# A two-layer MLP tail on TensorE: the output product moved out of the unit loop and done as seven Strassen passes

## The chip, the cores and the metric

The kernel runs on one core of one Trainium2 chip. Times are device microseconds of one execution; three runs of the kernel before are shown below. TensorE is the matmul engine, VectorE (DVE in the profile), ScalarE (ACT) and GpSimd (POOL) are the elementwise engines, SyncE (SP) issues all DMAs. All data is float32; the matmuls read operands of type float32r.

## The reference

```python
attn = coarse attention on 4-fold means, repeated, + banded local attention
x = attn as (2304 tokens, 512)
a = x @ w1; b = x @ w2                  # 512 -> 1024
h = a * b @ w3                          # 1024 -> 1024
y = h @ w_out                           # 1024 -> 512, first MLP
h2 = y @ w_in                           # 512 -> 2048
g = h2 * (1.0 / (1.0 + np.exp(-h2)))    # silu
out = g @ w_out2                        # 2048 -> 512
```

The change concerns the last three lines: `y`, 2304 tokens by 512, with `w_in` (512 by 2048) and `w_out` (2048 by 512) of the second MLP, called `w_in` and `w_out` from here on.

## The kernel before, in words

Every product of float32 accuracy is three matmuls (`PASSES`): each operand is split into a rounded high part (a cast to float32r) and a residual (operand minus high part, an elementwise subtraction of two SBUF operands), and high x high, residual x high and high x residual are added up in PSUM.

Up to about 109 us an opening written out by hand (`OPENING`) runs attention for the first heads and prepares the first weights. Then a list of `slots` is run, TensorE in that written order: groups of `ab` products (x with w1 and w2), `y` products, and the rest of attention between them. `y` is stored to DRAM (`ydram`). Beside it, 16 background units (`bg_steps`, lines 808 to 864; `plan` gives each step a slot) prepare `w_in` and `w_out` for the last stage: load, join two 32-bit words into one float, for `w_in` also form four Strassen sums (`mix`), cast to a high part (`high`, line 833), subtract (`rest`, line 837) and store both parts to DRAM (`wsd`, `wod`). In this part only TensorE's order is fixed by hand; steps on the other engines are put behind given instructions.

The last stage (lines 1003 to 1159) is written in a fixed order for all engines. Tokens come in `NT = 3` slabs of 768 (index `t`), two halves of 384 each; the 2048 middle columns in 8 blocks of 256 (index `p`). There are 24 units `u = 8 t + p`. `h_unit(u)` (line 1090) does one 2 x 2 Strassen product of a slab with a block of `w_in`: seven products (`CH`), each six matmuls of 384 columns, that is two contraction tiles times three passes. The operands of y are four blocks of the slab and four sums of them (`y_mix`, on GpSimd, line 919), cast on ScalarE (`y_high`, line 924) and with a residual on VectorE or GpSimd (`y_rest`, line 930). The operands of `w_in` are loaded per unit, already split (`wc_load`, lines 940 and 943). Each of the seven products starts a PSUM bank afresh; VectorE adds them up into `cf` and `cg` (line 1098), ScalarE takes the sigmoid (line 1063), VectorE multiplies and casts (lines 1069, 1072), GpSimd subtracts (line 1074). That gives `g` as two parts.

Between the products of a unit stand the output blocks of the unit before (`run_out`, `out_block`, line 1011): six blocks of 128 tokens times two halves, each three matmuls of 512 columns (line 1021) with `w_out` as the moving operand, added up over all p in six PSUM banks per slab. At the end of a slab the six banks are copied and stored (lines 1033 to 1041). The next slab of y is loaded in p = 1, mixed in p = 2 to 5, split in p = 7.

Products of the y sums to PSUM banks, and banks to engines, in the kernel before:

```python
            bank = s_tile if u or i == 6 else mm_tile if i < 4 else t_tile
            acc_full = bank(f"h{u}_{i}")
```

Of the kernel before, what the change touches and what calls it, by code (L numbers as in the profile page):

```python
# [8 lines left out]
F32 = mybir.dt.float32  # L9
# [65 lines left out]
def tile_model(ctx: ExitStack, tc: tile.TileContext, qk, vw, vr, w12, w3t, wo, wb, out):  # L75
# [14 lines left out]
    s_cb, s_late = ExitStack(), ExitStack()  # L90
# [5 lines left out]
    wsd = tc.dram_tile([8, P, 3584], F32, name="wsd")  # L96
    wod = tc.dram_tile([8, P, 2048], F32, name="wod")
# [710 lines left out]
    def bg_steps(n):  # L808
# [18 lines left out]
        def high(w):  # L827
            home = stg
            if late:
                n_res[0] += 1  # L830
                home = (stg, late[0])[n_res[0] % 2]
            hold["r"] = home.tile([P, 2, 1024], F32R, tag="res", name="res", bufs=1)[:, :, :w]
            nc.scalar.copy(hold["r"][:, 0], hold["f"][:, :w])

        def rest(w):
            r = hold["r"]
            nc.vector.tensor_tensor(
                out=r[:, 1], in0=hold["f"][:, :w], in1=r[:, 0].bitcast(F32), op=ALU.subtract
            )

        def store(where):
            nc.sync.dma_start(
                where.rearrange("p (l n) -> p l n", l=2), hold["r"].bitcast(F32)
            )

        def mix():
            f = hold["f"]
            a11, a12, a22, a21 = (f[:, 256 * i:256 * i + 256] for i in range(4))
            for out_, in0, in1, op in (
                (a22, a21, a22, ALU.add), (a21, a11, a21, ALU.subtract),  # L850
                (a11, a22, a11, ALU.subtract), (a12, a12, a11, ALU.subtract),
            ):
                nc.vector.tensor_tensor(out=out_, in0=in0, in1=in1, op=op)

        steps = [(0, first), (1, clamp), (3, low), (4, lambda: bg_load(n + 2))]
        if kind:
            steps += [(4, lambda: high(1024)), (5, lambda: rest(1024)),
                      (6, lambda: store(wod[p]))]
        else:
            steps += [(4, lambda: high(768)), (5, lambda: rest(768)),  # L860
                      (6, lambda: store(wsd[p, :, 0:1536])), (6, mix),
                      (8, lambda: high(1024)), (9, lambda: rest(1024)),
                      (10, lambda: store(wsd[p, :, 1536:3584]))]
        return steps
# [9 lines left out]
    late, n_res = [], [0]  # L874
# [13 lines left out]
    Y, YC, WC, WO, G, OUT = {}, {}, {}, {}, {}, {}  # L888

    CH = (("b11", 0, 0), ("b21", 0, 1), ("t2", 1, 0), ("t1", 1, 2),  # L890
          ("b22", 1, 1), ("t3", 1, 3), ("t4", 0, 2))
# [20 lines left out]
    def y_mix(t, i):  # L912
        b = Y[t]
        out_, in0, in1 = (("t1", "b12", "b11"), ("t2", "b22", "t1"),
                          ("t3", "b22", "b12"), ("t4", "t2", "b21"))[i]
# [18 lines left out]
    def wc_load(u):  # L934
        if u >= NUN:
            return
        p = u % 8
        t3 = wpool.tile([P, 2, 3, 256], F32R, tag="wB", name=f"wca{u}")
        t4 = wpool.tile([P, 2, 4, 256], F32R, tag="wB", name=f"wcb{u}")
        nc.sync.dma_start(  # L940
            t3.rearrange("p l c n -> p (l c n)").bitcast(F32), wsd[p, :, 0:1536]
        )
        nc.sync.dma_start(
            t4.rearrange("p l c n -> p (l c n)").bitcast(F32), wsd[p, :, 1536:3584]
        )
        WC[u] = (t3, t4)

    def wo_load(p):
        t = wpool.tile([P, 2, 2, 512], F32R, tag="wA" if p < 4 else "wC", name=f"wo{p}")
        nc.sync.dma_start(t.rearrange("p l f n -> p (l f n)").bitcast(F32), wod[p])  # L950
        WO[p] = t
# [6 lines left out]
    def open_y():  # L958
        s_late.close()
        s_stg.close()  # L960
        yp.append(pool(ctx, "yp", "left"))
        y_load(0)
# [4 lines left out]
    for i, k in ((0, 1), (1, 2), (3, 3), (2, 6), (4, 7), (5, 9), (6, 12)):  # L967
        at(bg_end + k, lambda i=i: y_high(0, i))
        at(bg_end + k + 1, lambda i=i: y_rest(0, i, True))
    at(end_b + 1, lambda: wc_load(0))  # L970
    at(end_b + 2, lambda: wc_load(1))
# [12 lines left out]
    with tc.manual_schedule(engines={T.PE}):  # L984
        for i, slot in enumerate(slots):
# [5 lines left out]
            if not opened and beat[0] >= END:  # L991
                assert not table and not [n for n in ops if n[0] != "z"], (table, list(ops))
                s_att.close()
                late.append(pool(s_late, "late", "left"))
# [221 lines left out]
```

## Time and profile before

| | |
|---|---|
| median of 3 runs | 838.88 us (836.98 to 840.41) |
| span of the profiled execution, first to last instruction | 834.7 us |
| an own device time of the profiled execution | not recorded; the median lies 4.2 us above its span |
| busy: TensorE / VectorE / ScalarE / GpSimd | 99% / 59% / 36% / 32% |
| last stage, from the first product with w_in | from about 453.6 us to the end |
| DMA | 149 MB in 44,032 packets, mean 179 GB/s |

Lines such as L1021 are lines of the kernel before. PE is TensorE's matmuls, PEld its weight loads, which run beside them; a matmul's duration holds its drain, which the next one overlaps, so back to back the spacing is less than the mean duration. An SPq row is a DMA being issued by SP.

### The profile page before, as it was taken

What the parts mean: (1) busy time and instruction counts of PE and PEld (TensorE: products, weight loads), DVE (VectorE), ACT (ScalarE), POOL (GpSimd) and SP (SyncE); (2) the same over time, 40 slices, a digit from 0 to 9 for tenths busy, and PEclk for the clock granted to TensorE, in tenths of its full rate; (3) what the DMA queues carried; (4) which work ended last, traced back from release to release, by engine and by line L of the source; (5) the groups of instructions that cost most, each with busy time, mean ns of one, the idle gap of its engine ahead of it and who ended that gap; (6) DMA issues with size and microseconds to landing.
All of it is one profiled execution on the core that took longest, in us unless ns stands there. A gap on an engine that the chain in (4) does not pass through costs nothing.

```text
span 834.7 us, 17445 instructions
## 1 busy us (share of the span) xinstructions
PE 824.6 (99%) x7126; PEld 736.5 (88%) x7126; DVE 494.4 (59%) x827; ACT 302.1 (36%) x881; POOL 269.6 (32%) x216
## 2 busy tenths in 40 slices
PE   8999999999999999999999999999999999999997
PEld 4555799999999999999999989989989989989986
DVE  7989896666747545476761534438534437534434
ACT  6588664544444534443331211123111123111111
POOL 3000233543535334231451523435223435222220
PEclk9999999999999999999999999999999999999999
DMA  9978754455565724429932864633863423823402
GB/s 313 377 202 265 232 170 153 146 200 189 167 227 165 253 96 165 145 92 332 375 130 75 296 248 146 225 134 97 243 164 95 170 90 97 242 90 95 170 2 75
DMA packets 44032, 149.16 MB, mean 179 GB/s; under 512 B 9136, under 2 KB 15792, under 8 KB 37808
## 3 DMA queue, kind: packets, MB, share of 16 engines
q1 hardware_dynamic: 43952, 148.05, 52.6%
q8 instruction: 56, 0.92, 0.5%
q14 instruction: 24, 0.20, 0.1%
HBM read 115.52 MB, written 32.51 MB: 177 GB/s over the span
## 4 chain that ended last, share of the span: by engine, by line
PE 92%; DMA 4%; DVE 3%; issue 1%; ACT 0%; SPq 0%; ACTq 0%
PE o L1021 24%; PE ab L665 23%; PE h L1110 21%; PE y L733 12%; PE wp L621 4%; PE ol L509 2%; DMA st<-w 2%; DMA qk<-qk 1%; PE s L402 1%; PE td L427 1%; PE od L487 1%; PE tl L457 1%; DMA lent<-wo 1%; PE sd L360 1%; DVE dec L191 0%
## 5 line engine op out<-in xcount | busy, mean ns | idle before, releaser
L1021 PE MATMUL o<-wo,g 128*128 128x512 f32 x864 | 221.1, 393 | 0.0
L1021 PEld LDWEIGHTS o<-wo,g 128*128 128x128 f32 x864 | 160.7, 188 | 25.4
L1074 POOL TENSOR_TENSOR g<-sg,g 128x768 fp32r<-128x768 f32 x46 | 84.9, 1845 | 228.4 <-DVE g L1072 206.8
L1110 PE MATMUL h<-yc,wcb 128*128 128x384 f32 x576 | 116.0, 337 | 0.0
L1110 PEld LDWEIGHTS h<-yc,wcb 128*128 128x128 f32 x576 | 103.2, 188 | 7.7
L707 POOL TENSOR_TENSOR c<-cf,c 128x320 fp32r<-128x320 f32 (+1 forms) x64 | 74.3, 1161 | 102.1 <-DVE c L702 95.9
L733 PE MATMUL y<-c,w_wC 128*128 128x320 f32 (+1 forms) x768 | 106.6, 296 | 0.0
L665 PE MATMUL ab<-x,w_wA 128*128 128x320 f32 (+1 forms) x768 | 106.3, 296 | 0.2 <-DVE w_wA L268 0.2
L665 PE MATMUL ab<-x,w_wB 128*128 128x320 f32 (+1 forms) x768 | 105.7, 296 | 0.0
L665 PEld LDWEIGHTS ab<-x,w_wB 128*128 128x128 f32 x768 | 102.1, 188 | 1.3 <-issue 0.4
L665 PEld LDWEIGHTS ab<-x,w_wA 128*128 128x128 f32 x768 | 101.6, 188 | 1.0 <-DVE w_wA L268 0.5
L733 PEld LDWEIGHTS y<-c,w_wC 128*128 128x128 f32 x768 | 101.9, 188 | 0.3
L1063 ACT ACTIVATE sg<-cf 128x768 f32<-128x768 f32 x24 | 20.3, 847 | 182.8 <-DVE cf L1098 182.8
L1110 PE MATMUL h<-yc,wca 128*128 128x384 f32 x432 | 83.1, 336 | 0.0
L1110 PEld LDWEIGHTS h<-yc,wca 128*128 128x128 f32 x432 | 76.6, 188 | 3.8
L683 DVE TENSOR_TENSOR cf<-ab,af 128x320 f32<-128x320 f32 (+1 forms) x64 | 28.9, 452 | 57.0 <-PE ab L665 37.0
L621 PE MATMUL wp<-w_wo,w_w 128*128 128x512 f32 x128 | 60.1, 602 | 0.3 <-DVE w_wo L191 0.2
L471 POOL TENSOR_TENSOR vr<-vr 72x512 f32<-72x512 f32 x11 | 16.0, 1454 | 120.0 <-DVE w_wB L268 84.1
L1063 ACT ACTIVATE sg<-cg 128x768 f32<-128x768 f32 x24 | 20.3, 847 | 88.3 <-DVE cg L1098 88.3
L1098 DVE TENSOR_TENSOR u<-h,u 128x384 f32<-128x384 f32 x48 | 26.6, 554 | 39.2 <-PE h L1110 39.0
L327 ACT ACTIVATE band<-band,sml 128x38 f32<-128x38 f32 x144 | 44.9, 319 | 5.3 <-DVE sml L418 5.2
L677 ACT COPY af<-ab 128x320 f32<-128x320 f32 (+1 forms) x64 | 25.3, 396 | 53.1 <-PE ab L665 53.0
(124 smaller groups left out, 1007.2 us busy)
## 6 DMA issues: line engine op xcount, KB each, us to landing
wcb<-wsd SPq DMA_DIRECT2D x24, 1024.0 KB
wca<-wsd SPq DMA_DIRECT2D x24, 768.0 KB
sw<-wb SPq DMA_DIRECT2D x32, 512.0 KB
qk<-qk SPq DMA_DIRECT2D x16, 579.0 KB
wsd<-res SPq DMA_DIRECT2D x8, 1024.0 KB
wod<-res SPq DMA_DIRECT2D x8, 1024.0 KB
wo<-wod SPq DMA_DIRECT2D x8, 1024.0 KB
st<-w SPq DMA_DIRECT2D x14, 512.0 KB
```

Of the source, the lines that this page charges most:

```text
L327: nc.scalar.activation(E[:, j, :], src[j], AF.Exp, bias=z[:, j:j + 1], scale=scale, accum_out=z[:, NQB + j:NQB + j + 1],)
L621: nc.tensor.matmul(wp_ps[half, j], lhsT=w3v[:, k, j * P:(j + 1) * P], rhs=wov[:, k, :], start=(gp == 0 and k == 0), stop=(gp == 3 and k == 1),
L665: nc.tensor.matmul(acc[:, :N], lhsT=wv[:, i, w, kk, :], rhs=X[b, h, kk][:, j, :], start=(n == 0), stop=(n == 11),)
L677: mark(nc.scalar.copy(af, C.pop(("ab", b, h, m, 0))[:, :N]))
L683: nc.vector.tensor_tensor(out=cf, in0=C.pop(("ab", b, h, m, 1))[:, :N], in1=C.pop(("af", b, h, m)), op=ALU.mult)
L707: mark(nc.gpsimd.tensor_tensor(out=c[:, 1], in0=C.pop(("cf", b, h, m)), in1=c[:, 0].bitcast(F32), op=ALU.subtract))
L733: nc.tensor.matmul(acc[:, :N], lhsT=WP[kf // 2][:, i, kf % 2, ec * P:(ec + 1) * P], rhs=c[:, j, :], start=(kf == 0 and n == 0), stop=(kf = ...
L1021: nc.tensor.matmul(acc, lhsT=g[:, a, j * P:(j + 1) * P], rhs=w[:, b, half, :], start=(p == 0 and half == 0 and n == 0), stop=(p == 7 and h ...
L1063: nc.scalar.activation(sg, c, AF.Sigmoid)
L1074: e.tensor_tensor(out=g[:, 1], in0=sg, in1=g[:, 0].bitcast(F32), op=ALU.subtract)
L1098: nc.vector.tensor_tensor(out=out_, in0=in0, in1=in1, op=op)
L1110: nc.tensor.matmul(acc, lhsT=wc[w][:, a, c, kt * P:(kt + 1) * P], rhs=y[:, b, kt, :], start=(n == 0), stop=(n == 5),)
```

## The change

The last stage becomes two parts.

First part: the 24 units run without output blocks between them. The seven products of a unit use three PSUM banks: products 0, 2, 4, 6 add into one (`X_`), 3 and 5 into another (`Y_`), 1 has a third (`Z_`); between them ScalarE or VectorE reads the running sum. The silu results `cf`, `cg` stay unsplit and are stored to DRAM (`gd`), with four sums of them that GpSimd makes (`S1` to `S4`, 384 columns each). `w_in` is stored unsplit by the background units and loaded once: 14 tiles of 1024 columns, each cast on ScalarE (`wc_high`) and subtracted on GpSimd (even) or VectorE (odd) (`wc_rest`). Tiles 0 to 3 are split before the last stage, 4 to 13 in units 0 to 5.

Second part: for each of seven Strassen passes, nine tiles of 128 rows; a tile is 24 matmuls of 256 columns. Operands are loaded unsplit (`a_load`, eight tiles ahead; `b_load`) and split on ScalarE and VectorE or GpSimd (`a_split`, four tiles ahead; `b_split`). Partial sums stand in SBUF (`U`, `oa`, `ob`); VectorE adds each pass to them. The first splits of this part stand in units 21 to 23. The pool `late` goes; `w_out` and `w_in` are stored unsplit (`store_plain`, `store_mixed`).

The core of the diff, in the order of the file:

```diff
-        def high(w):
...
-        def rest(w):
...
+        def mix(part):
+            q = [hold["f"][:, 256 * i:256 * i + 256] for i in range(4)]
...
+            for out_, in0, in1, op_ in todo[2 * part:2 * part + 2]:
+                nc.vector.tensor_tensor(out=out_, in0=in0, in1=in1, op=op_)
...
-    for i, k in ((0, 1), (1, 2), (3, 3), (2, 6), (4, 7), (5, 9), (6, 12)):
+    for i, k in ((0, 1), (1, 2), (3, 3), (2, 6), (5, 7), (4, 9), (6, 12)):
...
-    at(end_b + 1, lambda: wc_load(0))
-    at(end_b + 2, lambda: wc_load(1))
+    for s in range(8):
+        k = end_b + 1 + s // 2 if s < 4 else end_a + 1 + s // 4 - 1
+        at(k, lambda s=s: wc_load(s))
+        if s < 4:
+            at(k + 2, lambda s=s: wc_high(s))
+            at(k + 3, lambda s=s: wc_rest(s))
...
+    def halves(t, e):
+        def high():
+            nc.scalar.copy(t[:, 0], t[:, 1].bitcast(F32))
+        def rest():
+            e.tensor_tensor(
+                out=t[:, 1], in0=t[:, 1].bitcast(F32), in1=t[:, 0].bitcast(F32), op=ALU.subtract
+            )
+        return high, rest
...
+    def wc_rest(s, e=None):
+        halves(WC[s], e or (nc.vector if s % 2 else nc.gpsimd))[1]()
...
     def y_rest(t, i, e=None):
         d = YC[t, i]
+        e = e or (nc.vector if i % 2 else nc.gpsimd)
...
+        for i, (name, o) in enumerate(CH):
+            acc = (X_, Z_, X_, Y_, X_, Y_, X_)[i]
...
             if i == 0:
+                nc.scalar.copy(p1, X_)
             elif i == 1:
+                tt(cf[:, first], Z_, p1)
             elif i == 2:
+                nc.scalar.copy(u2, X_)
             elif i == 3:
+                nc.scalar.copy(p5, Y_)
             elif i == 4:
+                tt(cg[:, second], X_, p5)
+                nc.scalar.activation(sg[:, second], cg[:, second], AF.Sigmoid)
             elif i == 5:
+                tt(cf[:, second], Y_, u2)
+                nc.scalar.activation(sf, cf, AF.Sigmoid)
+                tt(cg[:, second], cg[:, second], sg[:, second], ALU.mult)
+                save(2, cg[:, second])
             else:
+                nc.scalar.activation(sg[:, first], X_, AF.Sigmoid)
+                tt(cf, cf, sf, ALU.mult)
+                tt(cg[:, first], X_, sg[:, first], ALU.mult)
...
+                tt(S1, cf[:, second], cg[:, second], ALU.add, g)
+                tt(S3, cf[:, first], cf[:, second], ALU.subtract, g)
+                tt(S2, S1, cf[:, first], ALU.subtract, g)
...
+                tt(S4, cg[:, first], S2, ALU.subtract, g)
...
+            for fn in extra.get(i, ()):
+                fn()
...
+            if t == 0:
+                todo = {0: (4, 5), 1: (6,), 2: (7, 8), 3: (9, 10), 4: (11, 12), 5: (13,)}
+                for k, s in enumerate(todo.get(p, ())):
+                    put((0, 3)[k], lambda s=s: wc_high(s), lambda s=s: wc_rest(s))
+            if t + 1 < NT:
+                if p == 1:
+                    put(6, lambda t=t: y_load(t + 1))
+                if 2 <= p < 6:
+                    put(6, lambda t=t, p=p: y_mix(t + 1, p - 2))
+                if p == 6:
+                    for i in range(2):
+                        put((0, 3)[i], lambda t=t, i=i: y_high(t + 1, i),
+                            lambda t=t, i=i: y_rest(t + 1, i))
+                if p == 7:
+                    for i in range(2, 7):
+                        put(i - 2, lambda t=t, i=i: y_high(t + 1, i),
+                            lambda t=t, i=i: y_rest(t + 1, i))
...
+            elif p == 5:
+                put(0, lambda: b_split(0, 0))
+                put(3, lambda: b_split(0, 1))
+                put(6, lambda: a_load(3), lambda: b_load(1))
+            elif p == 6:
+                put(0, lambda: a_split(0))
+                put(3, lambda: a_split(1))
+                put(6, lambda: a_load(4), lambda: a_load(5))
+            elif p == 7:
+                put(0, lambda: a_split(2))
+                put(3, lambda: a_split(3))
...
+        for m in range(7 * NP):
+            i, n = divmod(m, NP)
...
+            for p in range(8):
+                for k, (a, b) in enumerate(PASSES):
+                    nc.tensor.matmul(
+                        acc, lhsT=A[:, a, p, :], rhs=B_[i][p // 4][:, b, p % 4, :],
...
+            a_load(m + 8)
...
+            a_split(m + 4)
```

## Rows read from the trace of the kernel before

**Rows 1.** The page, busy time of the engines and share of the span
```profile
PE 824.6 (99%) x7126; PEld 736.5 (88%) x7126; DVE 494.4 (59%) x827; ACT 302.1 (36%) x881; POOL 269.6 (32%) x216
```

**Rows 2.** The chain that ended last, in order of time: start, length, work
```profile
433.99 8.48 PE ab L665 x72
442.47 11.31 PE y L733 x96
453.78 11.52 PE h L1110 x66
...
819.88 9.64 PE o L1021 x42
```

**Rows 3.** What TensorE waited for from 109 us on: total us, times, longest
```profile
PE ab L665 <- DVE w_wA L268: 0.2, 1, 0.2
```

**Rows 4.** Three unit periods, busy time of the instructions on h alone
```profile
508.08:523.74 15.66, 8.33 (x43) 7.51 (x43) 3.80 (x7) 0.48 (x1) 1.00 0.50 185
523.74:539.40 15.66, 8.33 (x43) 7.51 (x43) 3.79 (x7) 0.48 (x1) 1.00 0.52 187
539.40:555.06 15.66, 8.33 (x43) 7.51 (x43) 3.80 (x7) 0.48 (x1) 1.00 0.50 183
```

**Rows 5.** TensorE's widths: two timeline rows, then the busy PE, PEld of y
```profile
442.31 11.47 PE L733 MATMUL y<-c,w_wC 128*128 128x256 f32 x96
819.72 9.79 PE L1021 MATMUL o<-wo,g 128*128 128x512 f32 x42
442.31:453.62 11.31, 11.31 (x96) 11.26 (x96) 1.12 (x3) 1.00 0.07 25
```

**Rows 6.** Instructions by line and shape: busy us, mean ns
```profile
L1021 PE MATMUL o<-wo,g 128*128 128x512 f32 x864 | 221.1, 393 | 0.0
L1117 ACT COPY p<-h 128x384 f32<-128x384 f32 x24 | 11.5, 481 | 21.3 <-PE h L1110 21.3
L833 ACT CAST res<-dec 128x1024 fp32r<-128x1024 f32 x16 | 16.8, 1051 | 21.7 <-DVE dec L853 9.3 <-DMA wsd<-res 9.1 <-DVE res L837 2.4
L924 ACT CAST yc<-yr 128x768 fp32r<-128x768 f32 x12 | 9.7, 834 | 0.4 <-PE h L1110 0.4
L683 DVE TENSOR_TENSOR cf<-ab,af 128x256 f32<-128x256 f32 x32 | 13.4, 418 | 30.3 <-PE ab L665 18.0 <-PE tl L457 6.0 <-ACT dec L174 3.9
L539 POOL TENSOR_TENSOR x<-xf,x 128x256 fp32r<-128x256 f32 x11 | 8.5, 768 | 3.7 <-ACT x L535 3.7
```

**Rows 7.** Timeline at the start of the last stage
```profile
453.62 2.25 PE L1110 MATMUL h<-yc,wca 128*128 128x384 f32 x12
454.91 0.48 ACT L1117 COPY p<-h 128x384 f32<-128x384 f32 x1 [0.68 <-PE h L1110]
```

**Rows 8.** Timeline of the opening, a releaser's end and TensorE's start
```profile
23.31 1.23 DVE L191 SCALAR_TENSOR_TENSOR w_wo<-w_wo,lent 128x1024 int32<-128x1024 int32 x1
24.59 4.56 PE L621 MATMUL wp<-w_wo,w_w 128*128 128x512 f32 x10
```

**Rows 9.** Timeline of VectorE and of GpSimd, 412 to 414 and 566 to 575 us
```profile
412.52 1.22 DVE L837 TENSOR_TENSOR res<-dec,res 128x1024 fp32r<-128x1024 f32 x1
566.02 0.96 DVE L1069 TENSOR_TENSOR sg<-cf,sg 128x768 f32<-128x768 f32 x1
567.72 1.84 POOL L1074 TENSOR_TENSOR g<-sg,g 128x768 fp32r<-128x768 f32 x1 [7.10 <-DVE g L1072]
567.96 0.55 DVE L1098 TENSOR_TENSOR cg<-h,u 128x384 f32<-128x384 f32 x1
569.52 1.85 POOL L930 TENSOR_TENSOR yc<-t,yc 128x768 fp32r<-128x768 f32 x1
569.83 2.35 DVE L930 TENSOR_TENSOR yc<-t,yc 128x768 fp32r<-128x768 f32 x1
571.33 2.56 POOL L930 TENSOR_TENSOR yc<-yr,yc 128x768 fp32r<-128x768 f32 x1
572.11 2.60 DVE L1069 TENSOR_TENSOR sg<-cg,sg 128x768 f32<-128x768 f32 x1
```

**Rows 10.** DMA in two stretches: last columns the DMA share and GB/s
```profile
607.00:611.00 4.00, 4.00 (x22) 3.58 (x21) 0.71 (x2) 0.00 (x0) 0.00 (x0) 1.00 1.34 218
414.00:422.00 8.00, 8.00 (x62) 8.00 (x61) 2.17 (x6) 0.80 (x2) 2.97 (x4) 1.00 1.01 379
```

**Rows 11.** Timeline of the end, the last eviction
```profile
829.55 0.69 DVE L1033 COPY last<-o 128x512 f32<-128x512 f32 x1 [0.69 <-PE o L1021]
```

**Rows 12.** GpSimd's residuals of g, one line: durations min/median/max in ns
```profile
L1074 POOL TENSOR_TENSOR g<-sg,g x46: 1834/1846/1860, 463.1 to 807.5; 128x768 fp32r<-128x768 f32 x46
```

More of the change, by code (lines that the diff above doesn't have):

```diff
@@ L841, in store @@
[L841 to L863, printed above, removed]
@@ L864, in bg_steps @@
-        return steps
+        def mix(part):
+            q = [hold["f"][:, 256 * i:256 * i + 256] for i in range(4)]
+            if part == 0:
+                hold["r"] = stg.tile([P, 4, 256], F32, tag="res", name="res", bufs=2)
+            r = [hold["r"][:, i, :] for i in range(4)]
+            if kind:
+                todo = (
+                    (r[0], q[1], q[0], ALU.subtract), (r[1], q[3], r[0], ALU.subtract),
+                    (r[2], q[3], q[1], ALU.subtract), (r[3], q[2], r[1], ALU.subtract),
+                )
+            else:
+                todo = (
+                    (r[2], q[3], q[2], ALU.add), (r[3], q[0], q[3], ALU.subtract),
+                    (r[0], r[2], q[0], ALU.subtract), (r[1], q[1], r[0], ALU.subtract),
+                )
+            for out_, in0, in1, op_ in todo[2 * part:2 * part + 2]:
+                nc.vector.tensor_tensor(out=out_, in0=in0, in1=in1, op=op_)
@@ L866, in tile_model @@
+        return [
+            (0, first), (1, clamp), (3, low), (4, lambda: bg_load(n + 2)),
+            (4, lambda: mix(0)), (5, store_plain), (5, lambda: mix(1)), (6, store_mixed),
+        ]
     plan = {}
@@ L1090, in h_unit @@
[L1090 to L1106 removed]
+    b2.append(pool(ctx, "b2", "right", bufs=2))
@@ new lines, in rows, with store_out, temp @@
+    def rows(t, k):
+        return [64 * ORDER[SEQ[t][2 * k + i]] for i in range(2)]
+    def store_out(o, t, k, c0, c1):
+        r0, r1 = rows(t, k)
+        if r1 == r0 + 64:
+            nc.sync.dma_start(out[r0:r0 + 128, c0:c1], o)
+            return
+        nc.sync.dma_start(out[r0:r0 + 64, c0:c1], o[:64, :])
+        nc.sync.dma_start(out[r1:r1 + 64, c0:c1], o[64:, :])
+    def temp(tag, u, width=NH, bufs=1):
+        return b2[0].tile([P, width], F32, tag=tag, name=f"{tag}{u}", bufs=bufs)
@@ new lines, in h_unit, with b_load, a_load @@
+            for fn in extra.get(i, ()):
+                fn()
+    PR = ((0, 0), (1, 1), (4, 4), (3, 3), (5, 5), (6, 2), (2, 6))
+    NP = 9
+    A_, B_ = {}, {}
+    def b_load(i):
+        B_[i] = []
+        for k in range(2):
+            t = wpool.tile([P, 2, 4, 256], F32R, tag="wB", name=f"wo{i}_{k}")
+            nc.sync.dma_start(
+                t[:, 1].bitcast(F32), wod[:, 4 * k:4 * k + 4, PR[i][1], :]
+            )
+            B_[i].append(t)
+    def a_load(m):
+        if m >= 7 * NP:
+            return
+        i, n = divmod(m, NP)
+        t, j = divmod(n, 3)
+        d = wpool.tile([P, 2, 8, P], F32R, tag="wA" if m % 8 < 4 else "wC", name=f"ga{m}")
+        nc.sync.dma_start(
+            d[:, 1].bitcast(F32), gd[PR[i][0]][t][:, :, j * P:(j + 1) * P]
+        )
+        A_[m] = d
@@ L1150, in tile_model, with a_split, b_split @@
+    def a_split(m):
+        if m < 7 * NP:
+            high, rest = halves(A_[m], nc.vector if m % 2 else nc.gpsimd)
+            high()
+            rest()
+    def b_split(i, k):
+        high, rest = halves(B_[i][k], nc.vector)
+        high()
+        rest()
     E = mybir.EngineType
     with tc.manual_schedule(engines={E.PE, E.DVE, E.Activation, E.Pool, E.SP}):
+        for s in range(8, 14):
+            wc_load(s)
         for u in range(NUN):
-            h_unit(u)
-            assert not todo
@@ L1155, in tile_model, with put @@
-            todo.extend((u, half, j) for half in range(2) for j in range(6))
-        for _ in range(3):
-            next_chain()
-        assert not later
-        run_out(12)
+            t, p = divmod(u, 8)
+            ex = {}
+            def put(i, *fns):
+                ex.setdefault(i, []).extend(fns)
+            if t == 0:
+                todo = {0: (4, 5), 1: (6,), 2: (7, 8), 3: (9, 10), 4: (11, 12), 5: (13,)}
+                for k, s in enumerate(todo.get(p, ())):
+                    put((0, 3)[k], lambda s=s: wc_high(s), lambda s=s: wc_rest(s))
```

271 lines of the change are left out of this document (110 added, 161 removed).

## The prediction

> **What bounds the kernel now.** I read the engines' shares first: TensorE is busy 99% of the span and every other engine at most 59% [rows 1]. The chain of waits then shows TensorE alone from 434 us to the end [rows 2], and the list of what TensorE waited for has one entry of 0.2 us from 109 us on [rows 3]. So time is TensorE's instructions at their spacing, and the other engines matter only where TensorE comes to wait for them. In the last stage a unit (seven products with w_in, twelve output blocks of the unit before) takes 15.66 us, three times alike [rows 4]. The spacing of matmuls back to back is 11.31/96 = 0.1178 us at 256 columns, 11.52/66 = 0.1745 at 384 and 9.64/42 = 0.2295 at 512 [rows 2, 5]. A unit by these is 42 x 0.1745 + 36 x 0.2295 = 15.59, so there is no slack in it.
>
> **The change, part by part.** *Output product.* 864 matmuls of 512 columns go, 864 x 0.2295 = 198.3 us [rows 6]. In come 7 x 9 x 24 = 1512 of 256 columns, 178.1 us. Gain 20.2. The weight loads fill 11.26 of 11.31 us in the stretch of 256 columns [rows 5], but the spacing measured there already holds that. The 1008 matmuls with w_in stay: 7.33 us per unit, now with nothing between them.
>
> *Shorter background work and weight traffic.* The casts, the residuals and half of the store bytes of the background units leave engines that TensorE did not wait for [rows 3]: nothing gained. The casts and residuals that come back just before the last stage (four of each) are covered by queues with some 30 us to spare; if ScalarE stood still for one of the loads, TensorE might lose up to 4 us (two casts of 1.05 and a load of some 2). I take 0.
>
> *Three shared banks.* A product now adds to the bank of one two places before it, so TensorE waits for that bank's reader. ScalarE starts its copy 454.91 - (453.62 + 6 x 0.1745) = 0.25 us after the product [rows 7], the copy takes 0.48 [rows 6], and TensorE resumes 0.05 after a releaser ends (24.54 to 24.59) [rows 8]: 0.78. With VectorE's 0.56 it is 0.86. The one product in between covers 1.047. Cost 0; without that cover, about 0.9 us each time.
>
> *Work put behind product 3.* At eight places a cast and a residual stand on ScalarE and VectorE behind product 3, ahead of the VectorE sum that frees the bank for product 6. From the end of product 3: 0.25 + 0.48 + 1.05 (cast of 1024) + 0.05 + 1.22 (residual, [rows 9]) + 0.56 + 0.05 = 3.66, where product 6 could start after 2.09: TensorE stands 1.6 us. With 768 elements (0.84 and 0.96) it is 3.19, hence 1.1. What is queued behind it on VectorE is the whole rest of the unit.
>
> *VectorE against GpSimd.* A VectorE sum of two SBUF operands of 768 takes 0.96 alone, but 2.35 and 2.60 beside GpSimd sums, whose second is drawn out from 1.85 to 2.56; they alternate, a pair every 2.53 us [rows 9]. VectorE instructions with a PSUM operand stay at 0.55 beside GpSimd [rows 9]. So sums of two SBUF operands exclude one another, and each VectorE one costs GpSimd 2.53 - 1.85 = 0.68 (0.34 at 384, 0.91 at 1024). The Trainium skill, page "SBUF — State Buffer", section "SBUF: two separate sides", says the same pair of ports is locked for the whole instruction and the other side blocks fully; by that a pair would cost 1.85 + 0.96 = 2.81. The trace has 2.53 and decides; by the page's full lock the forecast below would be 849.7.
>
> *GpSimd in the first eight units.* The change gives GpSimd four sums of 384 per unit for the next pass. By 0.77 at 256 [rows 6] and 1.85 at 768 [rows 9] one is 1.04, so 4.15 per unit. With half of the w_in residuals (2.38 at 1024 on the same line), the four mixes of y (1.85) and half of the y residuals (1.85), the queue between the first sums and the y residual that product 2 of unit 8 needs is 7 x 4.15 + 4 x 2.38 + 4 x 1.85 + 2 x 1.85 = 49.7. VectorE's turns in that time: 7 units' silu products (1.02 each), four residuals of 1024, three of 768, 12.8. The sums of unit 0 start at 7.33 + 1.6 + 1.7 (silu) = 10.6. The end is 73.1, and product 2 of unit 8 should start at 8 x 7.33 + 2 x 1.05 = 60.7: TensorE comes out 12.4 us late. The 1.6, 1.1 and 1.3 us of the three waits behind product 3 in these units fall inside that. Lower end: no turns cost anything, GpSimd is done at 60.3, and the order alone costs 4.0. Upper end: VectorE's whole 0.96 is exclusive, 17.6 (12.8 x 0.96/0.68 = 18.0 of turns). I take 12.4, since the pair of rows is the same kind of work.
>
> *Units 8 to 23.* In the second eight, GpSimd has some 57 us of work and turns for 58.6, so no backlog grows. The five waits behind product 3 remain. Unit 14: the residual meets a y mix that starts at the same moment, 1.1 + 1.5 = 2.6. Unit 15: 1.1, 0.3 for a late cast, 0.6 for a sum in front, 2.0. Unit 21: 1.6 + 0.7 = 2.3. Units 22 and 23: a GpSimd residual of 2.38 runs when VectorE is ready, 1.6 + 1.8 = 3.4 each. Sum 13.7. Lower end (VectorE always first) 7.3, upper (a whole GpSimd instruction in front each time) 16.6.
>
> *Seven passes.* A tile of 24 matmuls lasts 2.83 us. ScalarE's cast 1.05, VectorE's residual of 1.22 every second tile with one or two evictions of 0.42, GpSimd's 2.38 every second tile: all fit, and splits run four tiles ahead, loads eight. The load is 524 KB in rows of 512 bytes. Rows of 256 bytes went at 218 GB/s, longer ones at 379 [rows 10], so it takes 1.4 to 2.4 us of 2.83. Cost 0 with w_out and stores beside it at any rate up to the middle; see the third rival. SP issues a load and at most two stores per tile, behind waits that the eight tiles cover.
>
> *Tail.* The last eviction falls from 0.69 [rows 11] to 0.42 (256 columns, [rows 6]): -0.3.
>
> *Sum.* -20.2 - 0.3 + 12.4 + 13.7 = +5.6 on the profiled span of 834.7, that is 840.3. The median of runs, 838.88, stands 4.2 above this span, so 844.5 in the measure of the runs. About 0.5% (4.2 us) is what a measurement can tell from no change.
>
> **Rivals.** *The order costs, the queue doesn't (faster).* If VectorE's turns cost GpSimd nothing, only waits by order are left: -20.5 + 4.0 + 7.3 = -9.2, 829.7. For it: 46 GpSimd residuals in the last stage now all take 1.83 to 1.86 [rows 12]; against it: those seldom meet VectorE's sums of two SBUF operands, and where they do both are drawn out. It decides if GpSimd ends the first eight units less than some 6 us late; halfway is 837. Chance 0.24.
>
> *All hidden.* The product behind covers everything: 838.9 - 20.5 = 818.4. Against it stands the plain order on VectorE: 0.05.
>
> *Loads of the seven passes bind (slower still).* At 218 GB/s for all of it, 33.0 MB of sums, 5.2 MB of w_out and 4.7 MB of output take 197 us against 178; six tiles loaded ahead are 14 of that, so TensorE waits about 5: 849.5. The upper ends of the two GpSimd terms, 844.5 + 5.2 + 2.9 = 852.6, lie near it, and both at once give 857.6. These upper ends are what the page's full lock, named above, would do; the pairs at 2.53 bear it out little, and it has 0.05. The skill's page "DMA: Bandwidth & Descriptors", section "Specifications", puts full rate at 512 bytes and above, by which this would cost nothing; no row of this trace has such loads. Chance together, the 0.05 among it, 0.13.
>
> *The change doesn't do what it says* would be a spacing at 256 columns above 0.118; the y stretch, with other weights at each matmul, speaks against it, and I give it nothing of its own.
>
> **How the numbers follow.** The forecast, GpSimd's queue late by 10 to 15 us and VectorE's waits as listed, spans 840 to 852 with 0.58: 0.13 of it within 0.5% of 838.9 (up to 843.1), 0.45 above. The first rival spans 826 to 839: 0.14 faster than 834.7, 0.10 within. Hidden: 0.05 faster. The last: 0.13 slower. That makes faster 0.19, same 0.23, slower 0.58. The range 830 to 857 leaves out the hidden case, half of the lower part of the first rival and the end of the last.
>
> **What would show it.** Units of the first third should take 8 to 10 us and not 7.33, and TensorE should wait at product 2 of unit 8 for a GpSimd residual of y. Units 14, 15, 21, 22 and 23 should have a gap of 2 to 3.5 us before product 6, released by VectorE. GpSimd should be near 90% busy in the first third, with drawn-out instructions there. The seven passes should take 178 us without a wait. A unit time of 7.33 in the first third would make the forecast wrong at its largest term; gaps in the seven passes released by loads would show the third rival.

## The result and the profile after

The changed kernel takes 844.19 us in the median of 16 runs (840.63 to 849.27), the kernel before 838.71 (16 runs): ratio 1.006, 95% interval [1.004, 1.008]. The forecast was 844.5. It is slower, by about the amount forecast, and TensorE waits mostly where the forecast has it wait. That the sum comes out this close is partly luck: both terms of gaps and the tail were 1.5 to 3 us too high each, and one effect, a fall of TensorE's clock, was not in it at all.

The profiled execution took 845.13 us, its span is 843.3. First the engines' busy time from the page of the changed kernel:

```profile
PE 811.1 (96%) x7774; PEld 754.7 (89%) x7774; DVE 523.3 (62%) x821; ACT 393.1 (47%) x1020; POOL 387.6 (46%) x303
```

TensorE fell from 99% [rows 1] to 96%: it now waits. Two views show where. The first is the list of what TensorE waited for from 440 us on (engine, line and work waited for: total us, times, longest). The second has four stretches of the last stage (from:to, length, busy us of PE, PEld, DVE, ACT, POOL, then granted clock, DMA share, GB/s): units 0 to 8 up to product 1 of unit 8, from there into unit 16, the rest of the units, the seven passes:

```profile
PE hx L1054 <- DVE cg L1033: 15.9, 8, 2.8
PE hx L1054 <- POOL yc L932: 4.2, 1, 4.2
PE hx L1054 <- ACT u L1064: 0.9, 1, 0.9
```

```profile
456.94:523.50 66.56, 60.70 (x346) 59.33 (x345) 48.16 (x55) 40.50 (x67) 55.78 (x35) 1.00 0.57 193
523.50:596.20 72.70, 65.28 (x360) 63.61 (x359) 42.95 (x54) 32.00 (x59) 59.40 (x47) 0.98 0.58 190
596.20:658.60 62.40, 54.55 (x309) 52.87 (x307) 36.27 (x49) 29.15 (x50) 37.68 (x35) 1.00 0.76 253
658.60:840.10 181.50, 181.50 (x1513) 181.40 (x1512) 92.05 (x106) 75.28 (x82) 85.25 (x34) 1.00 0.80 229
```

A unit without a wait takes 7.29 us, 42 matmuls 0.1735 apart, so 24 units would take 174.9; they take 658.60 - 456.94 = 201.7. The passes have no wait in them. Against [rows 2, 3], where TensorE waited 0.2 us, these 26.8 us are the loss of the last stage.

The timeline of the changed kernel at unit 8 (start, length, engine, line; in brackets how long it stood and for whom) shows the forecast place, product 2 behind a y residual of GpSimd. The row below the timeline is the stretch behind the gap, with its granted clock, 0.58:

```profile
523.31 1.22 PE L1054 MATMUL hz<-yc,wc 128*128 128x384 f32 x6
524.37 0.51 PE L1054 MATMUL hx<-yc,wc 128*128 128x384 f32 x2
526.28 0.99 POOL L1033 TENSOR_TENSOR S<-cg,S 128x384 f32<-128x384 f32 x1
527.24 1.80 POOL L932 TENSOR_TENSOR yc<-t,yc 128x768 fp32r<-128x768 f32 x1
529.09 0.96 PE L1054 MATMUL hx<-yc,wc 128*128 128x384 f32 x4 [4.22 <-POOL yc L932]
529.89 2.03 PE L1054 MATMUL hy<-yc,wc 128*128 128x384 f32 x6
531.72 1.98 PE L1054 MATMUL hx<-yc,wc 128*128 128x384 f32 x6
```

```profile
529.50:532.50 3.00, 3.00 (x13) 3.00 (x12) 0.00 (x0) 0.96 (x2) 3.00 (x2) 0.58 0.32 115
```

GpSimd works through its queue without a break (28.8 of the 29 us from 500 on), and TensorE stands 4.2 us. Behind the gap six matmuls last 2.03 and 1.98 us where the product before it took 1.22: they start 0.320 us apart, not 0.1735, the spacing at half clock (1.2 in place of 2.4 GHz). Ten of them cost 1.5 us. Nothing in the trace of before shows such a stretch.

Units 6 and 7 lose another 2.4 and 2.7 us, at product 6, for a sum of VectorE. There GpSimd's lag comes by way of VectorE. The tiles `cf` and `cg` share four buffers, enough for two units, and GpSimd is a unit late, so the first sum of unit 6 stands until GpSimd has read the `cf` of unit 4. The timeline of unit 6, then what VectorE waited for from the start of the stage to 530 us:

```profile
508.65 0.56 DVE L1033 TENSOR_TENSOR cf<-hz,p 128x384 f32<-128x384 f32 x1 [2.38 <-POOL S L1033]
511.03 2.35 PE L1054 MATMUL hx<-yc,wc 128*128 128x384 f32 x12 [2.20 <-DVE cg L1033]
```

```profile
DVE cf L1033 <- POOL S L1033: 5.2, 3, 2.4
```

And unit 22, one of the waits behind product 3, in the timeline:

```profile
642.59 1.05 ACT L941 CAST ga<-ga 128x1024 fp32r<-128x1024 f32 x1
643.07 2.36 POOL L944 TENSOR_TENSOR ga<-ga 128x1024 fp32r<-128x1024 f32 x1
643.67 2.84 DVE L944 TENSOR_TENSOR ga<-ga 128x1024 fp32r<-128x1024 f32 x1 [2.87 <-ACT ga L941]
646.43 0.55 DVE L1033 TENSOR_TENSOR cg<-hx,p 128x384 f32<-128x384 f32 x1
647.03 2.19 PE L1054 MATMUL hx<-yc,wc 128*128 128x384 f32 x11 [2.80 <-DVE cg L1033]
```

Cast, residual (1.22 alone [rows 9], here 2.84 beside GpSimd), sum, product 6: the chain of the forecast.

### The profile page after: what moved, and what is told of

Its sections match the earlier page's. It is cut to its first block, busy times and chain, and to the rows that moved or that the text cites. A ratio compares the mean times of both kernels' runs of the same rounds, so it can differ in the third digit from the quotient of the medians.

```text
span 843.3 us, 19587 instructions
## 1 busy us (share of the span) xinstructions
PE 811.1 (96%) x7774; PEld 754.7 (89%) x7774; DVE 523.3 (62%) x821; ACT 393.1 (47%) x1020; POOL 387.6 (46%) x303
## 5 line engine op out<-in xcount | busy, mean ns | idle before, releaser
L1190 PE MATMUL q<-wo,ga 128*128 128x256 f32 x1512 | 181.6, 283 | 0.0
L1190 PEld LDWEIGHTS q<-wo,ga 128*128 128x128 f32 x1512 | 181.6, 192 | 0.0
L1054 PE MATMUL hx<-yc,wc 128*128 128x384 f32 x576 | 114.8, 340 | 21.1 <-DVE cg L1033 15.9
L944 POOL TENSOR_TENSOR ga<-ga 128x1024 fp32r<-128x1024 f32 x32 | 86.0, 2691 | 84.5 <-ACT ga L941 84.5
L1054 PEld LDWEIGHTS hx<-yc,wc 128*128 128x128 f32 x576 | 100.7, 189 | 25.8 <-DVE cg L1033 19.1
L941 ACT CAST ga<-ga 128x1024 fp32r<-128x1024 f32 x63 | 65.3, 1049 | 48.7 <-DMA ga<-gd 42.8
L944 DVE TENSOR_TENSOR ga<-ga 128x1024 fp32r<-128x1024 f32 x31 | 51.1, 1649 | 19.5 <-ACT ga L941 16.7
L1054 PE MATMUL hy<-yc,wc 128*128 128x384 f32 x288 | 58.7, 339 | 0.0
L1054 PEld LDWEIGHTS hy<-yc,wc 128*128 128x128 f32 x288 | 51.4, 190 | 0.0
L1033 POOL TENSOR_TENSOR S<-cf,cg 128x384 f32<-128x384 f32 x24 | 25.7, 1071 | 43.2 <-DVE cf L1033 43.2
```

Source lines behind the costliest of these rows:

```text
L941: nc.scalar.copy(t[:, 0], t[:, 1].bitcast(F32))
L944: e.tensor_tensor(out=t[:, 1], in0=t[:, 1].bitcast(F32), in1=t[:, 0].bitcast(F32), op=ALU.subtract)
L1033: (e or nc.vector).tensor_tensor(out=out_, in0=in0, in1=in1, op=op_)
L1054: nc.tensor.matmul(acc, lhsT=WC[s][:, a, c, kt * P:(kt + 1) * P], rhs=y[:, b, kt, :], start=(n == 0 and i in (0, 1, 3)), stop=(n == 5), sk ...
L1190: nc.tensor.matmul(acc, lhsT=A[:, a, p, :], rhs=B_[i][p // 4][:, b, p % 4, :], start=(p == 0 and k == 0), stop=(p == 7 and k == 2),)
```

## The experiments

Theory: GpSimd's queue, drawn out by VectorE, makes TensorE late by unit 8; the order on VectorE, written for banks of their own, makes the waits in the other two thirds. Rival: the order alone. The fall of the clock is a question too. For it I use (1 - mean clock) x span, the full-clock time that a run lost at most; falls in the opening are in it as well. Diffs are against the changed kernel unless said.

### c0_again: the changed kernel once more

No edit.

> The changed kernel once more, with a profile of its own, to tell what belongs to the program from what belongs to one execution. Theory (GpSimd's queue plus the order written for three products): the same 12 or so us of waits in the last third of the units, the same 4 us wait of TensorE at product 2 of unit 8 and the stretch of half clock behind it; the 3.3 us by which the last stage began late in the first profile is of one execution and is mostly gone; time within 841 to 849. Rival (the 3.3 us belong to the program): the last stage begins 3 us or more later than in the kernel before again. Rival (the drop of the clock is chance and has nothing to do with the gap): the clock stays full after the gap, or falls somewhere else.

843.26 us. Its profiled execution has a span of 838.0, 5.3 less than the first. What TensorE waited for from 440 us on, and the clock in a stretch of unit 7:

```profile
PE hx L1054 <- DVE cg L1033: 15.8, 8, 2.8
PE hx L1054 <- POOL yc L932: 3.0, 1, 3.0
```

```profile
518.00:521.00 3.00, 2.80 (x9) 2.80 (x10) 2.33 (x4) 2.46 (x4) 3.00 (x3) 0.50 0.00 0
```

The waits belong to the program. The 3.3 us ahead of the last stage don't: it begins at 454.0, before at 453.6 [rows 7]. The clock fell again, but behind the gap of unit 7 and not that of unit 8: somewhere else, as the second rival allows, yet still behind a gap. The six timed runs have mean clocks of 0.992 to 0.998, the shortest span (838.0) at 0.998 and the longest (844.0) at 0.992.

### e1_order: the order alone

```diff
-   put((0, 3)[i], lambda: y_high(t + 1, i), lambda: y_rest(t + 1, i))
+   put((0, 3)[i], lambda: y_high(t + 1, i))
+   put((0, 6)[i], lambda: y_rest(t + 1, i))
```

(and the same for tile 5 of `w_in`, `y_rest` 5, `b_split(0, 1)`, `a_split(1)` and `a_split(3)`.)

> The changed kernel with every VectorE residual that stood behind product 3 of a unit moved behind product 6; the casts stay. Theory (the queue of GpSimd in the first third, the order in the other two): the waits of units 14, 15, 21, 22 and 23 go, 12.3 us in the profile, and the 1.3 of unit 0; some 10.5 of them come back as time, since the residuals then lie beside the next unit's first product; the gap at product 2 of unit 8 stays, as it is ended by GpSimd: 832 to 834. Rival (the order alone makes the loss, GpSimd's lag would follow the same waits): the gap at unit 8 goes as well, about 827. Rival (the waits only move, the residual now holds back the next unit's S2 or sums): 841 to 845.

837.32 us, ratio to the kernel before 0.999 [0.997, 1.001]; 6 to 7 less than the changed kernel. TensorE's waits from 440 us on:

```profile
PE hx L1054 <- POOL yc L932: 6.4, 2, 4.8
PE hx L1054 <- DVE cg L1033: 4.8, 5, 1.9
PE q L1194 <- POOL ga L944: 1.2, 1, 1.2
```

VectorE's entry falls from 15.8 to 4.8, GpSimd's at unit 8 stays and grows. By the starts of the matmuls the gaps up to product 2 of unit 8 still add up to 10.3 us, against 10.7 and 9.6 in the two traces of the changed kernel, while of the 12.2 us of gaps in units 9 to 23 only 3.6 are left (2.0 of them in unit 15), and 1.2 came in the first pass. So the two causes are separate, as the theory has it. The band (832 to 834) was too low: two stretches at half clock, 26 matmuls, took 3.8 us.

### e2_vector: GpSimd's queue

```diff
-   put((0, 3)[k], lambda: wc_high(s), lambda: wc_rest(s))
+   put((0, 3)[k], lambda: wc_high(s))
+   put((0, 6)[k], lambda: wc_rest(s, nc.vector))
```

on top of e1_order's edit.

> As the run before, and all residuals of w_in tiles 4 to 13 on VectorE (five of them were GpSimd's), the second of a unit behind product 6. Theory with taken turns (an instruction of VectorE beside one of GpSimd takes longer, by the pair of 2.53 us): GpSimd's queue loses 4 x 2.38 us = 9.5 until unit 8, VectorE has 4 x 0.91 = 3.6 more, so the 4.2 us gap at unit 8 shrinks to under 1 and the waits of units 6 and 7 go: 5.9 us less than the run before, 826 to 829, and no stretch of half clock. Rival (no turns, GpSimd's queue alone counts): 9.5 less, 823 to 825. Rival (order alone): no difference to the run before.

832.14 us, ratio 0.993 [0.991, 0.995]: 5.2 below e1_order, where turns said 5.9, none 9.5 and the order alone 0. That rival is out. But 5.2 isn't all gaps: by the mean clocks the runs of e1_order lost at most 4.0 us and these 1.9, and in the two traces the gaps up to product 2 of unit 8 fell from 10.3 to 6.4, 3.9 us and not 5.9. The gap at unit 8 itself went, and VectorE no longer waits for GpSimd at `cf`. TensorE's waits from 440 us on, then VectorE and GpSimd in unit 7:

```profile
PE hx L1054 <- DVE cg L1033: 6.8, 6, 2.0
PE hx L1054 <- POOL yc L932: 1.7, 3, 1.4
```

```profile
519.30 1.02 POOL L1033 TENSOR_TENSOR S<-cf,cg 128x384 f32<-128x384 f32 x1 [0.90 <-DVE cf L1033]
519.62 1.52 DVE L932 TENSOR_TENSOR yc<-yr,yc 128x768 fp32r<-128x768 f32 x1
520.28 1.71 POOL L1033 TENSOR_TENSOR S<-cf 128x384 f32<-128x384 f32 x1
521.53 1.28 DVE L932 TENSOR_TENSOR yc<-t,yc 128x768 fp32r<-128x768 f32 x1
521.96 1.71 POOL L1033 TENSOR_TENSOR S<-S,cf 128x384 f32<-128x384 f32 x1
```

A GpSimd sum of 384 that begins before VectorE's residual of 768 takes 1.02, as it does alone, and the residual takes 1.52 in place of 0.96. The next sum, which begins beside the residual, takes 1.71: 0.69 more, the price of a turn that the forecast took from the pair of 2.53 (0.68) [rows 9]. A lock for the whole instruction, as the Trainium skill's page "SBUF — State Buffer", section "SBUF: two separate sides", has it, would make it 1.02 + 0.96 = 1.98; the trace has 1.71 and decides.

### e4_gpsimd: more in GpSimd's queue

```diff
-   lambda: wc_rest(s))
+   lambda: wc_rest(s, nc.gpsimd))
```

> The changed kernel with the five VectorE residuals of w_in tiles 5, 7, 9, 11 and 13 put on GpSimd as well, nothing else. Theory (GpSimd's queue decides unit 8, with turns): four more residuals of 2.38 us in GpSimd's queue until then, four of 0.91 fewer beside it: TensorE later by 5.9, 848 to 851. Rival (no turns): later by 9.5, 852 to 855. Rival (the order of VectorE alone makes the loss): the wait of unit 0 goes and nothing comes: 841 to 843.

850.12 us, ratio 1.015 [1.013, 1.017]: in the theory's band, but only half for its reason. By the starts of the matmuls the gaps up to product 2 of unit 8 add up to 12.7 us, against 10.7 and 9.6 in the two traces of the changed kernel: 2 to 3 more, not 4.6 (5.9 less the wait of unit 0, which went). Matmuls at half clock number 33 in place of 10 and 7, and the mean clock of the four timed runs is 0.988: at most 10.0 us lost, 5.3 in c0_again. So the extra work on GpSimd came out partly as gaps and about as much through the clock. VectorE's waits for GpSimd at `cf` in these units grow with that work: none in e2_vector's trace, 5.2 us in the changed kernel's, 9.9 here.

### e6_fill: TensorE kept busy in the gap

```diff
+   if u == 8 and i == 2:
+       for _ in range(24):
+           nc.tensor.matmul(fill, lhsT=WC[0][...], rhs=YC[t, 0][...], start=True, stop=True)
```

> The changed kernel with 24 idle matmuls of 384 columns (about 4.2 us, their result is not read) in front of product 2 of unit 8, in the place where TensorE stood idle 4.2 us for GpSimd. The output is unchanged. Theory (the stretch of half clock behind the gap is the answer to TensorE's standing still there): the gap is filled, the granted clock stays 1.00 behind it, and products 3 and 4 of unit 8 take 1.04 us each in place of 1.83, so 1.6 us less in the profile, and as much or more in the median, with the spread of the runs narrower: 838 to 843. Rival (the clock falls for another reason, at the same time or elsewhere): the same time as the changed kernel or up to 1 us more, the same spread and mean clock.

843.04 us, 0.2 below c0_again: no difference that the runs can tell. In the timeline the products behind the filled place take 1.20:

```profile
524.93 4.35 PE L1054 MATMUL fill<-yc,wc 128*128 128x384 f32 x24
530.58 1.20 PE L1061 MATMUL hy<-yc,wc 128*128 128x384 f32 x6
```

That settles nothing: in c0_again the same products take 1.20 behind the gap that was left open (3.0 us). And here the clock fell behind the gaps of units 6 (2.4 us) and 22 (3.0) instead. The run is inconclusive: one gap of five was filled.

### v1_all and v2_mix_gpsimd: the work laid out anew

```diff
+   at(NA - 6 + 2 * (s // 6), lambda: wc_high(s))              # s = 4 to 7, before the stage
+   at(NA - 5 + 2 * (s // 6), lambda: wc_rest(s, nc.vector))
...
+   put(0, lambda s=8 + p: wc_high(s)); put(6, lambda s=8 + p: wc_rest(s, nc.vector))
...
-   nc.gpsimd.tensor_tensor(out=b[out_], ...)                  # y_mix; v1 only
+   nc.vector.tensor_tensor(out=b[out_], ...)
...
+   put((1, 6, 6, 6, 4)[i - 2], lambda: y_rest(t + 1, i, nc.gpsimd if i == 6 else nc.vector))
```

> A version for the time, from what the first runs showed. The splits of w_in tiles 4 to 7 move into the last 8 us of the stage before (VectorE and ScalarE stand there), tiles 8 to 13 are split one a unit, their residuals, the subtractions for the next third and all but one of its residuals are VectorE's and stand behind product 6, and the loads for the first output pass are issued one unit earlier. GpSimd keeps the four sums of a unit. Theory (GpSimd's queue with turns, and the order): of the 24 us of TensorE's waits in the 24 units at most 3 are left, no gap is over 1 us, the granted clock stays 1.00, and what is left is 174.9 + 181.4 against 375.7 + 2 of the kernel before: 816 to 823. Rival (VectorE, now with 5.4 of 7.3 us a unit and drawn out beside GpSimd, becomes the bound of the first third): waits of products behind cg come back, 4 to 8 us, 824 to 830. Rival (the clock falls without a gap as well): the waits go, but the mean clock stays at 0.993 and the time at 822 to 827.

> The version before with one thing put back: the four subtractions for the next third stay on GpSimd. Theory with turns: GpSimd has 4.1 + 2.2 us of 7.3 in units 2 to 5 and is drawn out by what VectorE does beside it, so its sums fall behind by 4 to 6 us by unit 6; little of that reaches TensorE, as no residual but one is GpSimd's: 0 to 3 us more than the version before. Rival (no turns): the same as the version before within 0.5. Rival (GpSimd's lag alone makes the waits, wherever the residuals are): 6 us or more above the version before.

v1_all 839.47 us (ratio 1.001 [0.999, 1.003]), v2_mix_gpsimd 832.88 (0.993 [0.991, 0.995]). Both theories fell by sign or size: moving the four subtractions (mixes) to VectorE cost 6.6 us. The timeline of v1_all in unit 3 says why:

```profile
483.20 0.96 DVE L917 TENSOR_TENSOR t<-yr 128x768 f32<-128x768 f32 x1 [3.43 <-DMA yr<-ydram]
484.54 0.55 DVE L1038 TENSOR_TENSOR cg<-hx,p 128x384 f32<-128x384 f32 x1
485.15 2.35 PE L1059 MATMUL hx<-yc,wc 128*128 128x384 f32 x12 [2.76 <-DVE cg L1038]
```

It isn't VectorE's load, as my rival had it: the subtraction waits for the load of the next slab, and in VectorE's fixed order the sum that frees the bank stands behind it. On GpSimd the same wait has no one behind it that TensorE needs soon. In unit 11 it happens again: the subtraction stands 6.2 us for a DMA and TensorE 3.8.

### e7_gap: a gap on purpose

```diff
+   for _ in range(9 if u == 12 else 0):      # in v1_all, behind product 0
+       nc.scalar.copy(p1, X_)
```

> The version of the first run of this call with one gap made on purpose: in unit 12 ScalarE copies the first product of the unit nine times more into the same place, so that product 2, which adds to that bank, can't start; nothing else changes. The nine copies take 9 x 0.42 to 0.48 us, so TensorE stands some 3 to 3.5 us longer there. Theory (the granted clock falls as an answer to TensorE's standing still): behind the gap the granted clock is 0.50 for some us and the products take 1.92 instead of 1.04 us: 4 to 7 us more than the version without the gap, where the gap alone is 3 to 3.5. Rival (the falls have another cause): the clock stays 1.00 and the time is 3 to 3.5 us more.

845.43 us, 6.0 above v1_all. The timeline of unit 12:

```profile
559.85 4.56 ACT L1067 COPY p<-hx 128x384 f32<-128x384 f32 x9
564.47 2.29 PE L1059 MATMUL hx<-yc,wc 128*128 128x384 f32 x6 [3.36 <-ACT p L1067]
566.55 1.75 PE L1059 MATMUL hy<-yc,wc 128*128 128x384 f32 x6
568.14 1.21 PE L1059 MATMUL hx<-yc,wc 128*128 128x384 f32 x6
```

TensorE stood 3.4 us, and the next matmuls are at half clock (2.29 and 1.75 where 1.21 is normal). Of the 6.0 us 3.4 is the gap; the mean clock went from 0.995 to 0.991, worth 3.1 (7.46 - 4.33). The theory's sum fits. One reserve: a gap of 3.7 us just before, in unit 11, was there already, and in this trace half clock stands behind it too.

### v3_spread, v4_loads, v5_rest4: what was left

v3_spread against v2_mix_gpsimd:

```diff
+   todo = {0: (8, 9), 1: (10, 11), 2: (12,), 3: (13,)}
...
+   put((0, 1)[i], lambda: y_high(t + 1, i)); put((1, 2)[i], lambda: y_rest(t + 1, i, nc.vector))
...
-   put((1, 6, 6, 6, 4)[i - 2], ...
+   put((1, 2, 6, 6, 4)[i - 2], ...
...
-       high, rest = halves(A_[m], nc.vector if m % 2 else nc.gpsimd)
+       high, rest = halves(A_[m], nc.vector if m % 2 or m == 4 else nc.gpsimd)
```

> From the last version but one (subtractions for the next third on GpSimd) three things moved: tiles 8 to 13 of w_in are split two a unit in units 0 and 1 and one in units 2 and 3, before GpSimd's subtractions pile up; the residuals of the next third are spread, two a unit over units 6, 7 and 8 in place of two, one and four, so that never more than two stand on VectorE ahead of the sum for cg that TensorE waits for; and the residuals of the third and fifth left operand of the output passes go from GpSimd to VectorE. Theory (what is left are the two engines' turns: where the solo times of both add up to more than a unit's 7.29 us, the VectorE queue runs late): the 2.4 us gap near unit 8 and the 2.3 near unit 16 shrink under 1 us, the 1.7 us at the start of the output passes goes, the clock stays at 1.00 more often: 825 to 829, against 832.9. Rival (the sum of both engines' work in units 5 to 8, not its place, sets the loss): gaps of the same sum in other places, 831 to 834.

830.33 us, ratio 0.990 [0.987, 0.994]: between the theory's band and the rival's, and by time not clearly below v2_mix_gpsimd. The gap near unit 8 fell from 2.4 to 1.1 us, that near unit 16 from 2.1 to 1.1. The largest that remained was one wait in the passes, in the timeline:

```profile
651.97 11.63 SPq L1118 DMA_DIRECT2D ga<-gd  x8
656.59 1.05 ACT L941 CAST ga<-ga 128x1024 fp32r<-128x1024 f32 x1 [7.09 <-DMA ga<-gd]
657.71 2.34 POOL L944 TENSOR_TENSOR ga<-ga 128x1024 fp32r<-128x1024 f32 x1 [6.19 <-ACT ga L941]
660.11 2.29 PE L1201 MATMUL q<-wo,ga 128*128 128x256 f32 x9 [2.04 <-POOL ga L944]
```

v4_loads issues two loads ahead of the last four stores and moves the residual of the seventh left operand to VectorE; v5_rest4 puts one residual back on GpSimd:

```diff
+   if u == NUN - 1: a_load(6); a_load(7)      # before S1 to S4; v4
...
-       high, rest = halves(A_[m], nc.vector if m % 2 or m == 4 else nc.gpsimd)
+       high, rest = halves(A_[m], nc.vector if m % 2 or m in (4, 6) else nc.gpsimd)    # v4
...
-   put((1, 2, 6, 6, 4)[i - 2], ... nc.gpsimd if i == 6 else nc.vector)
+   put((1, 2, 2, 6, 4)[i - 2], ... nc.gpsimd if i in (4, 6) else nc.vector)    # v5
```

> The version with spread residuals, and the loads of the seventh and eighth left operand of the output passes are issued in the last unit, ahead of the stores of its four sums on SP's queue, in place of behind them; the residual of the seventh goes to VectorE. Nothing else. Theory (the gap of 2.4 us at 20 us into the passes, which ends with a residual of GpSimd behind a load, is a load held up in SP's queue behind stores that wait for GpSimd's sums): the gap goes, and the stretch of half clock behind it: 185.3 us of passes become 181.5, 2 to 4 us less than the version before, 826 to 828.5. Rival (the load is late for its data, the last unit's store): the gap stays, 830.

> The version of the run before, and one more residual of the next third, the fifth, goes from VectorE back to GpSimd, behind product 2 of the last unit of a third. Theory with turns: 2.15 us of GpSimd for 0.72 of VectorE is 1.4 more of both together in a stretch where they are already full: 1 to 3 us slower over the two places. Rival (no turns, VectorE's queue alone holds up products here): 1 to 2 us faster.

v4_loads 826.41 us (0.985 [0.981, 0.988]), in the theory's band: the wait went, the passes took 181.3 in place of 185.3. The loads alone are enough for it: the cast that the load released began 10.5 us into the passes, in v3_spread 16.3, and TensorE had waited 2.0. TensorE's waits from 440 us on:

```profile
PE hx L1057 <- DVE cg L1036: 2.9, 4, 1.0
PE hx L1057 <- DVE yc L932: 1.0, 2, 0.5
PE hy L1057 <- DVE yc L932: 0.7, 2, 0.4
```

With no wait over 1.0 us the mean clock of its six runs is 0.999. v5_rest4 took 825.52: the theory of turns said slower by 1 to 3, but what TensorE lost in the 24 units fell from 9.2 to 7.7 us. A miss: the medians are 0.9 apart and the runs overlap (824.64 to 829.92 and 823.37 to 831.16), so neither a gain nor a loss is shown by time, and the two traces have smaller gaps and not larger ones. That the place in VectorE's queue counted here, and not the sum of both engines, fits them but wasn't tested apart.

### v6_pairs: the 120.0 ns

```diff
-   for k, (a, b) in enumerate(PASSES):
+   for k, (a, b) in enumerate(((0, 0), (0, 1), (1, 0))):      # on v5_rest4
```

> The version of the run before with the three partial products of every output block in another order: high x high, high x rest, rest x high, so that two matmuls in a row take the same left operand, where before the left operand changed with each. The output differs by rounding alone. It asks why the matmuls of the output passes come every 120.0 ns, where the 256-column ones of the stage before come every 113 to 119. Theory (the weight load that stands before every matmul, at 100% busy, sets the 120 ns, whichever operand it loads): 120.0 again, the passes take 181.3 us, the time stays within 0.5% of the run before. Rival (changing the left operand costs the 2 to 7 ns): the spacing of one matmul in three falls to 113 to 118, 1 to 3.5 us less in the passes.

824.89 us, ratio to the kernel before 0.983 [0.980, 0.985], the lowest median here; v4_loads, v5_rest4 and v6_pairs can't be told apart by time. The passes' matmuls (first and last start), v5_rest4 and then v6_pairs:

```profile
L1202 PE MATMUL q<-wo,ga x1512: 277/283/290, 644.7 to 826.0; 128*128 128x256 f32 x189
```

```profile
L1202 PE MATMUL q<-wo,ga x1512: 280/283/287, 639.0 to 820.3; 128*128 128x256 f32 x189
```

181.3 us both times, 120.0 ns a matmul: changing the left operand is not what costs. Why the y products come at 117.8 [rows 2, 5] stays open.

## Why the prediction was right, and where it wasn't

**The sum.** Gaps and half clock are read from the starts of the matmuls; the rest from the last stage's start, the 24 units, the passes and the tail, against the kernel before (last stage from 453.62 [rows 7], 24 x 15.66 = 375.8 [rows 4], tail 834.7 - 453.6 - 375.8 = 5.3):

| term | forecast | first profile | c0_again |
|---|---|---|---|
| front | 0 | +3.3 | +0.4 |
| output product | -20.2 | -19.5 | -19.5 |
| units 0 to 8, gaps | +12.4 | +10.7 | +9.6 |
| units 9 to 23, gaps | +13.7 | +12.2 | +11.6 |
| half clock in the units | none | +1.5 | +1.0 |
| other small gaps in the units | none | +2.4 | +2.2 |
| tail | -0.3 | -2.0 | -2.0 |
| span | +5.6 | +8.6 | +3.3 |

**GpSimd's queue**, the forecast's main term, was right in engine and in size to 2 to 3 us: e1_order leaves it, e2_vector takes 3.9 us of its gaps away, e4_gpsimd adds 2 to 3. Its picture of the way there was wrong. Units of 8 to 10 us in the first third were announced, but units 1 to 5 take 7.3 us, and apart from the 1.3 of unit 0 all the lateness falls on three gaps in units 6 to 8. Only the last, 4.4 us, stands at the forecast place; the other two, 2.4 and 2.7 where the forecast had 1.1 and 1.3 by order alone, are at product 6. GpSimd's lag reaches TensorE in two ways: where something TensorE needs stands in GpSimd's queue, and where VectorE waits for a buffer that GpSimd still reads. The second was not in the forecast.

**Waits behind product 3** came in units 0, 14, 15, 21, 22 and 23: 1.3, 1.7, 1.8, 2.5, 3.0 and 3.0 in the first profile, for 1.6, 2.6, 2.0, 2.3, 3.4 and 3.4. Of the 2.5 in unit 21, 1.0 is at product 4: there ScalarE's copy stands behind a cast that waited 1.9 us for a load of `w_out`, a wait by order that the forecast didn't have. e1_order takes 8.6 of the 12.2 us in units 9 to 23 away by order alone.

**Output product.** The step "864 x 0.2295 = 198.3" was mis-sized: between other products these matmuls were worth 375.8 - 174.9 = 200.9. So was "1512 ... 178.1": the spacing is 120.0 and not 117.8, 181.4. The two errors nearly cancel.

**Tail.** "-0.3" counted the last eviction alone; the time behind the last matmul fell from 5.3 to 3.3. What else got shorter there wasn't taken apart.

**From span to median.** Of the "4.2 above this span" 1.8 are there in every run (device time less span is 1.7 to 1.9 in the kernel before, 1.8 to 2.1 in the changed one), and the rest says that this execution was 2.4 us shorter than the median one. To add the difference of the spans to the median was right all the same.

**The clock** was missing. By their mean clocks the 16 runs lost at most 5.9 us each on average, the runs of the kernel before 1.2 (17 runs of c0_again's call): up to 4.7 of the 5.5 us between the medians; how much of it lies in the last stage only a trace tells. Without front and half clock the two profiles stand 3.8 and 1.9 us above the span before (8.6 - 3.3 - 1.5 and 3.3 - 0.4 - 1.0), where +5.6 was forecast. So the mechanism was right in the main, but the number came out this close by luck: terms that were 2 to 4 us too high together stood against a clock that was left out.

**Rivals.** "The order costs, the queue doesn't" is out by e1_order and e2_vector; "all hidden" by the 21 us that TensorE waits; "loads of the seven passes bind" by the passes, which have no wait at 229 GB/s, more than the 218 of [rows 10]. The front, set to 0, came out at 0.4 and 3.3: of the 2.9 us between the two traces 2.1 are the wait of the opening's first products for a load (3.3 and 1.2 us), which differs from execution to execution.

## What to carry to other kernels

When products that had banks of their own come to share one, every instruction in front of the reader of that bank is on TensorE's path: put background work behind the reader and never a wait for a load in front of it, and give the slow engine only work that nobody needs soon. Here the 20 us of matmuls saved were given back in gaps; with the order mended the same change is 1.7% faster than the kernel before.

## What the runs showed of the hardware

A gap can cost twice. In the last stages of the 13 traces of the changed kernel and its variants there are 15 stretches at half clock, each within 1.6 us behind a gap of TensorE; the gaps were 2.0 to 4.9 us long, others up to 3.1 had none behind them, and in the four traces without such a stretch no gap was over 2.2. The stretches last 2 to 5.5 us. The openings show the same: in seven of these traces the clock fell around a wait of 2.8 to 4.1 us for a load, in two others a wait of 2.6 or 3.3 had no fall. In the opening of v5_rest4, where TensorE stood 4.1 us, the clock of the 20 us around it fell to 0.74:

```profile
PE s L405 <- DMA qk<-qk: 4.4, 2, 4.1
```

```profile
20.00:40.00 20.00, 15.88 (x197) 8.87 (x196) 12.76 (x21) 8.08 (x20) 0.00 (x0) 0.74 1.02 360
```

Two runs of one program so differ by several us with the same instructions: which gap is answered by the clock changes from run to run, and the profile of one run shows only its own.
